# Head 0's queries transposed straight from fp32, and the first mask rows copied in another order

## The chip, the cores and the metric

The kernel runs on one NeuronCore of a Trainium2 chip. Five engines work side by side, each through its own list of instructions in order: TensorE (PE in the profile; its weight loads are PEld), VectorE (DVE), ScalarE (ACT), GpSimd (POOL) and SyncE (SP, which here only issues DMAs). They wait for one another through semaphores. Matrix products go to PSUM, from where VectorE or ScalarE copy them to SBUF. The metric is the device time of one execution in microseconds; three runs of the kernel before gave a median of 210.62 us (210.41 to 210.62).

## What is computed

Block-sparse attention (4 batches, 8 heads, 768 positions, head size 64; blocks of 32 positions) followed by a gated MLP. Cut to what matters:

```python
scores = q @ k.T / sqrt(D)
mask = |blk_i - blk_j| <= 1, or first/last block row or column, or block sampled for that row
attn = softmax(where(mask, scores, -1e9))
x = attn @ v                               # heads side by side: (4, 768, 512)
h = relu(x @ w_in); u, v = halves of h
v_n = (v - mean(v)) / sqrt(var(v) + 1e-6)
v_s = w_spatial @ v_n + b_spatial          # over positions
out = (u * v_s) @ w_out
```

## The kernel before

The 768 positions of a head are held as 6 chunks of 128 (position p*6 + c lies in row p of chunk c). `kq` has one slab for each of 8 heads: in partitions 0 to 63 the transposed keys (columns 0 to 767) and queries (columns 768 on, `Q_`), in partitions 64 and up the mask as extra rows: the keys' side is a one-hot code of the block, the queries' side the row of that block's mask, so that one matrix product gives scores and mask together. `qcols(t)` are the query columns of one third (two chunks, 256 columns).

Heads are taken in pairs. The first batch is worked off in *slots*: slot s makes the transposed scores of a piece (`qk_unit`, L387 to L420), one exponential on ScalarE (L410, L420) turns them into weights, and some slots later `av_unit` multiplies them with v. Score tiles use the PSUM tag `sc` (two buffers of two banks), the first-slot extra `ps_f` and the transposes a pair of banks that `moe_tag()` hands out in turn, `ps_av` and `psq` the tag `av` (two buffers). Slot 0 is head 0 with the first third of queries, made in two halves with an exponential each (L407, L410); slot 1 is head 0 with the second third, slot 2 head 0 with the last two key chunks for both thirds, slots 3 to 5 the same for head 1; from slot 6 on come pairs 1 to 3. The order on each engine is the order in which the program text issues the work: `tc.manual_schedule()`, no planner. `at`, `pre` and `late` hang further work on slots: `second` and `third` (L331, L337) transpose the rest of pair 0, `tr_first(p)` and `tr_rest(p)` pairs 1 to 3.

The start, which the change touches:

- DMAs: ScalarE's queue brings keys (four chunks) and then queries (four chunks) of head 0 as fp32 (L140, L141). SP's queue brings the other two chunks of keys, then head 1's keys and queries (L143 to L145), then pairs 1 to 3 and the first weights in the order of `ORDER`.
- GpSimd makes index patterns (`iota`), the bf16 identity (L169), the ones beside v (L171) and zeros in head 1's first query columns (L173); then it casts to bf16 head 0's queries (L245), the rest of pair 0 (L246 to L248), copies mask rows (L301, L302), and casts what `ORDER` brings (`casts`, L321).
- ScalarE casts head 0's first keys (L243), copies the keys' mask rows from slab 1 to slab 0 (L244), and then the queries' mask rows of the first two thirds from PSUM (`mask_rows`, L268, called at L290 and L298), with a copy of mask rows into head 2 between them (L291).
- VectorE builds the mask, copies transposed keys and queries from PSUM into `kq` (`split0`, L280: one half of a bank's partitions, two chunks at a time) and copies mask rows to other heads (`rows`, L236).
- TensorE runs 26 small products on zeros (`filler`), transposes head 0's first keys (`head`, L274), makes the mask rows, transposes head 0's queries into `psq` (L294), and starts slot 0.

The cast for pair 0 also reorders chunks, so that chunk pairs (0,2) and (1,3) are transposed together and each half of the partitions then holds two neighbouring chunks, one third of the queries.

Of the kernel before, what the change touches and what calls it, by code (L numbers as in the profile page):

```python
# [10 lines left out]
FP32 = mybir.dt.float32  # L11
# [15 lines left out]
def kernel(  # L27
# [16 lines left out]
    nc = tc.nc  # L44

    B, H, S, D = q.shape
# [16 lines left out]
    TC = NCH // NT  # L63
    TW = TC * 128
# [5 lines left out]
    const = ctx.enter_context(tc.tile_pool(name="const", bufs=1))  # L70
    work = ctx.enter_context(tc.tile_pool(name="work", bufs=1))
    psum = ctx.enter_context(tc.tile_pool(name="psum", bufs=1, space=bass.MemoryType.PSUM))
    ctx.enter_context(tc.manual_schedule())

    ident = const.tile([128, 128], BF16)
    warm = const.tile([128, 128], BF16)
    w_in_t = const.tile([128, NDM, DFF], BF16)
    w_out_t = const.tile([128, NDH, DM], BF16)
# [4 lines left out]
    kq = const.tile([128, H, 2 * S], BF16, name="kq")  # L83
    NVV = 6
    vv = [const.tile([128, 2, NCH, VA], BF16, name=f"vv{s}") for s in range(NVV)]
    MR = slice(D, KR)
    MX = slice(D, 128)
    K_, Q_ = slice(0, S), slice(S, 2 * S)

    def qcols(t0, n=1):  # L90
        return slice(S + t0 * TW, S + (t0 + n) * TW)


    st = {}
# [6 lines left out]
    H0, H1, BOTH = slice(0, 1), slice(1, 2), slice(0, 2)  # L101
    ALLC, C01, C03, C45 = slice(0, NCH), slice(0, TC), slice(0, 2 * TC), slice(2 * TC, NCH)
# [12 lines left out]
    def nat0_view():  # L115
        return nat[0].rearrange("p c h d -> p (c h d)").rearrange("p (h x) -> p h x", h=2)

    def cast(p, nm, eng, hs=BOTH, cs=ALLC):
        if nm == "v":
            dst = vv[p % NVV][:, hs, cs, 0:D]  # L120
        else:
            if p not in nat:
                nat[p] = work.tile([128, 2 * NCH, 2, D], BF16, tag="nat", bufs=4, name="nat")
            c0 = 0 if nm == "k" else NCH
            dst = nat[p][:, c0 + cs.start:c0 + cs.stop].rearrange("p c h d -> p h c d")[:, hs]
        src = st[nm, p].rearrange("p h (c d) -> p h c d", d=D)[:, hs, cs]
        if p == 0 and nm != "v":
            dst = nat0_view()[:, hs, (c0 + cs.start) * D:(c0 + cs.stop) * D]
            if cs is not C45:
                dst = dst[:, 0].rearrange("p (i t d) -> p t i d", t=2, d=D)  # L130
                src = src[:, 0].rearrange("p (t i) d -> p t i d", t=2)
            else:
                dst = dst.rearrange("p h (c d) -> p h c d", d=D)
        if eng is nc.scalar:
            nc.scalar.activation(out=dst, in_=src, func=AF.Copy)
        else:
            eng.tensor_copy(out=dst, in_=src)  # L137
# [23 lines left out]
    def iota(out, pattern, base, mult):  # L161
        nc.gpsimd.iota(out, pattern=pattern, base=base, channel_multiplier=mult,
                       allow_small_or_imprecise_dtypes=True)
# [2 lines left out]
    iota(edge[MR], [[0, 1]], 1 - NB, 2)  # L166
    iota(hot[MX], [[2, NCH], [2 * NCH, 128]], 1 - BLK, -2 * BLK)
    iota(col[MR], [[0, NR], [1, NB]], 0, 0)
    make_identity(nc, ident)  # L169
    for s in range(NVV):  # L170
        nc.gpsimd.memset(vv[s][:, :, :, D:VA], 1.0)  # L171
    nc.gpsimd.memset(mhalf, -0.5)
    nc.gpsimd.memset(kq[0:D, 1, 0:TW], 0.0)  # L173

    wps = psum.tile([128, 512], FP32, tag="av", bufs=2)

    def filler(n, to):
        for _ in range(n):
            nc.tensor.matmul(out=to[:, 0:128], lhsT=warm, rhs=warm, start=True, stop=True)
# [28 lines left out]
    PL, DV = nc.gpsimd, nc.vector  # L208
# [4 lines left out]
    def act_copy(o, i):  # L213
        nc.scalar.activation(out=o, in_=i, func=AF.Copy)
# [21 lines left out]
    def rows(hs, cs, eng=nc.vector):  # L236
        src = kq[MX, 0:1, cs].to_broadcast([MX.stop - MX.start, hs.stop - hs.start, cs.stop - cs.start])
        if eng is nc.scalar:
            nc.scalar.activation(out=kq[MX, hs, cs], in_=src, func=AF.Copy)
        else:  # L240
            eng.tensor_copy(out=kq[MX, hs, cs], in_=src)

    cast(0, "k", nc.scalar, H0, C03)  # L243
    act_copy(kq[MX, 0, K_], kq[MX, 1, K_])  # L244
    cast(0, "q", PL, H0, C03)  # L245
    cast(0, "k", PL, H0, C45)  # L246
    cast(0, "k", PL, H1)
    cast(0, "q", PL, H1, C03)  # L248
# [4 lines left out]
    def moe_tag():  # L253
        moe_tags.rotate(1)
        if moe_tags[0] in held:
            moe_tags.rotate(1)
        return moe_tags[0]

    def bank(nm="ps", tag=None):
        return psum.tile([128, 1024], BF16, tag=tag or moe_tag(), bufs=2 if tag else 1, name=nm)  # L260
# [7 lines left out]
    def mask_rows(ps, t, copy, h=0, rs=slice(0, KR)):  # L268
        nc.tensor.matmul(out=ps[:, 0:TW], lhsT=bm[rs], rhs=kq[rs, h, t * TW:(t + 1) * TW],
                         start=True, stop=True)  # L270
        copy(kq[MX, 0, qcols(t)], ps[0:MX.stop - MX.start, 0:TW])


    def head(ps, h, c0, n, at=0):  # L274
        for i in range(0, n, 2):
            nc.tensor.transpose(out=ps[:, at + i * 64:at + (i + 2) * 64],
                                in_=nat0_view()[:, h, (c0 + i) * D:(c0 + i + 2) * D],
                                identity=ident)

    def split0(ps, h, c0, n, t, copy=dve_copy):  # L280
        w = n * 64
        copy(kq[0:D, h, c0 * 128 + t * w:c0 * 128 + (t + 1) * w], ps[t * D:(t + 1) * D, 0:w])

    K4, K2, Q4 = (0, 2 * TC), (2 * TC, NCH - 2 * TC), (NCH, 2 * TC)
# [3 lines left out]
    rows(slice(3, 4), K_)  # L288
    filler(FILL2[0], wps)
    mask_rows(psum.tile([128, 1024], FP32, tag="sc", bufs=2, name="mq"), 0, act_copy, 1)  # L290
    rows(slice(2, 3), slice(0, 512), nc.scalar)  # L291
    filler(FILL2[1], wps)
    psq = bank("psq", "av")
    head(psq, 0, *Q4)  # L294
    split0(psq, 0, *Q4, 0)
    split0(ps0, 0, *K4, 1)
    filler(FILL2[2], wps)
    mask_rows(psum.tile([128, 512], FP32, tag=moe_tag(), bufs=1, name="mq"), 1, act_copy, rs=MR)  # L298
    split0(psq, 0, *Q4, 1)
    rows(slice(4, 6), K_)  # L300
    rows(H1, qcols(0, 2), PL)  # L301
    rows(slice(2, 3), slice(512, S), PL)  # L302

    ORDER = ("k1 q1a v00 v01 k2 q2a v1 k3 q3a v2 q1b q2b r v3 q3b q0c w00 w01 w02 w03 w10 w12 w11 w13").split()
    PIECE = {"k": {}, "v": {}, "q": {}, "a": {"cs": C01}, "b": {"cs": C25}, "c": {"cs": C45},
# [592 lines left out]
```

## Time and profile before

| | |
|---|---|
| median of three runs | 210.62 us (210.41 to 210.62) |
| the profiled execution's own time | 210.04 us |
| its span, first to last instruction | 208.3 us |
| granted TensorE clock, mean | 1.000 |
| chain that ended last, by engine | PE 87%, DVE 4%, ACT 4%, DMA 2% |
| queries of head 0 land | 4.34 us |
| first score product starts | 5.68 us |
| first exponential starts | 6.11 us |

Times inside the execution are microseconds from the start of the span. In lines of the timeline the first two numbers are start and length; `x4` says that four instructions are merged in the line, and the bracket how long the engine was idle before it and what ended that. In the two lines of slices each digit is the busy share of a fortieth of the span in tenths. `nat` is the bf16 copy of keys and queries, `st_q`, `st_k`, `st_v` are the landed fp32 tiles, `ps` and `psq` PSUM tiles, `mq` the product that makes mask rows, `a_all` the exponentials.

### The profile page before, as it was taken

To read this page: it belongs to the slowest core of one execution; us is meant where nothing else is said; L and a number is where in the kernel's file an instruction comes from. 1 tells how busy PE (TensorE), PEld (TensorE's weight loads), DVE (VectorE), ACT (ScalarE), POOL (GpSimd) and SP (SyncE) were. 2 spreads that over 40 slices of the span, in tenths; PEclk is the share of its full clock that TensorE was granted. 3 is DMA by queue.
4 is the path that set the end of the run, shared out by engine and by line. 5 is a ranking of instruction groups with operands and counts; after the bars stand their busy time and mean duration, and the time that the engine had idled before them with its cause. 6 is when DMAs were issued, how large, how long until landed. Compare 5 with 4: busy or idle time off the path is not lost.

```text
span 208.3 us, 5489 instructions
## 1 busy us (share of the span) xinstructions
PE 201.0 (97%) x2203; PEld 138.0 (66%) x2225; DVE 146.8 (70%) x315; ACT 168.4 (81%) x222; POOL 89.4 (43%) x186
## 2 busy tenths in 40 slices
PE   6899999999999999999999999999999999999993
PEld 6599888777766776667556676667665567445551
DVE  6888776989876766575975585456875666576871
ACT  6899999999999999989899878889899884266021
POOL 6888989767927964006757600006210000013000
PEclk9999999999999999999999999999999999999999
DMA  5999899999999999499987920499402010610016
GB/s 143 338 362 357 275 383 270 206 247 389 253 253 308 259 300 208 139 199 386 292 176 206 139 41 0 164 189 335 75 0 41 0 37 4 250 57 0 0 70 232
DMA packets 53053, 39.48 MB, mean 190 GB/s; under 512 B 33956, under 2 KB 47652, under 8 KB 53028
## 3 DMA queue, kind: packets, MB, share of 16 engines
q1 hardware_dynamic: 52596, 38.74, 70.0%
q10 hardware_dynamic: 432, 0.39, 0.6%
q8 instruction: 17, 0.28, 0.5%
q14 instruction: 8, 0.07, 0.1%
HBM read 24.77 MB, written 6.29 MB: 149 GB/s over the span
## 4 chain that ended last, share of the span: by engine, by line
PE 87%; DVE 4%; ACT 4%; DMA 2%; issue 1%; POOL 0%; ACTq 0%
PE ps L428 21%; PE ps_moe L630 17%; PE ps_moe L561 13%; PE ps_av L476 12%; PE ps L415 7%; PE ps_av L458 4%; PE ps_t L561 4%; PE ps_t L630 4%; PE ps_sc L630 2%; ACT a_all L420 2%; DVE stats L594 2%; DVE vn L185 2%; DMA st_q<-in_q_dram 2%; PE ps_sc L561 1%; PE ps L263 1%
## 5 line engine op out<-in xcount | busy, mean ns | idle before, releaser
L431 ACT ACTIVATE a_all<-ps 128x768 bf16<-128x768 f32 x144 | 113.4, 812 | 13.8 <-PE ps L428 6.2
L428 PE MATMUL ps<-kq 128*128 128x512 bf16 (+1 forms) x288 | 70.3, 326 | 0.3
L476 PEld LDWEIGHTS <-a_all 128*128 128x128 bf16 x864 | 46.6, 98 | 19.0
L476 PE MATMUL ps_av<-vv,a_all 128*128 128x65 bf16 x864 | 51.1, 194 | 0.1
L428 PEld LDWEIGHTS <-kq 128*128 128x128 bf16 x288 | 27.9, 97 | 23.6
L137 POOL CAST nat<-st_k 128x256 bf16<-128x256 f32 (+3 forms) x37 | 17.7, 509 | 38.7 <-DMA st_k<-in_k_dram 38.7
L420 ACT ACTIVATE a_all<-ps 128x1024 bf16<-128x1024 f32 x35 | 33.5, 1027 | 0.3
L630 PE MATMUL ps_moe<-w_spt,vn 128*128 128x512 bf16 (+1 forms) x144 | 33.1, 325 | 0.0
L598 POOL TENSOR_SCALAR std<-mv 128x3 f32<-128x3 f32 (+1 forms) x9 | 3.4, 376 | 48.7 <-DVE mv L595 48.5
L661 DVE TENSOR_TENSOR sb<-ps_moe,b_row 128x512 f32<-128x512 f32 x18 | 12.4, 690 | 14.5 <-PE ps_moe L630 14.2
L630 PE MATMUL ps_moe<-xt,w_in_t 128*128 128x256 bf16 (+1 forms) x108 | 21.7, 299 | 0.2
L415 PE MATMUL ps<-kq 128*128 128x256 bf16 x135 | 20.8, 275 | 0.8 <-DVE kq L211 0.6
L561 PE MATMUL ps_moe<-w_in_t,xt 128*128 128x512 bf16 x65 | 20.2, 378 | 0.2
L137 POOL CAST vv<-st_v 128x256 bf16<-128x256 f32 (+2 forms) x37 | 18.5, 533 | 3.9 <-DMA st_v<-in_v_dram 3.8
L137 POOL CAST nat<-st_q 128x256 bf16<-128x256 f32 (+2 forms) x41 | 19.2, 496 | 1.6 <-DMA st_q<-in_q_dram 1.5
L561 PE MATMUL ps_moe<-w_out_t,un 128*128 128x512 bf16 x64 | 19.4, 378 | 0.2
L441 DVE TENSOR_TENSOR xn<-ps_av,rc 128x384 bf16<-128x384 f32 (+1 forms) x36 | 18.5, 513 | 1.4 <-DVE rc L440 0.2
L664 DVE TENSOR_TENSOR un<-sb,un 128x512 bf16<-128x512 f32 x24 | 17.4, 727 | 1.5
L630 PEld LDWEIGHTS <-vn 128*128 128x128 bf16 x192 | 15.5, 97 | 4.4
L594 DVE BATCH_NORM_STATS2 stats<-vn 128x6 f32<-128x512 bf16 x24 | 16.5, 688 | 1.5 <-ACT vn L589 0.9
L211 DVE COPY osb<-ps_moe 128x512 f32<-128x512 f32 x12 | 8.3, 689 | 11.2 <-PE ps_moe L561 9.3
L211 DVE COPY kq<-tt 64x1536 bf16<-64x1536 bf16 x24 | 15.4, 641 | 0.6 <-DMA tt<-nat 0.2
(94 smaller groups left out, 241.6 us busy)
## 6 DMA issues: line engine op xcount, KB each, us to landing
out_dram<-osb SPq DMA_DIRECT2D x23, 256.0 KB, 2.1
st_k<-in_k_dram SPq DMA_DIRECT2D x15, 384.0 KB, 4.6
st_v<-in_v_dram SPq DMA_DIRECT2D x15, 384.0 KB, 6.2
st_q<-in_q_dram SPq DMA_DIRECT2D x12, 384.0 KB, 4.9
ws_f<-in_moe_w_spatial_dram SPq DMA_DIRECT2D x6, 384.0 KB, 5.5
w_f<-in_moe_w_in_dram SPq DMA_DIRECT2D x8, 256.0 KB, 6.3
w_f<-in_moe_w_out_dram SPq DMA_DIRECT2D x4, 256.0 KB, 5.4
st_q<-in_q_dram SPq DMA_DIRECT2D x3, 256.0 KB, 6.9
```

The costliest lines, as they stand in the source:

```text
L137: eng.tensor_copy(out=dst, in_=src)
L211: nc.vector.tensor_copy(out=o, in_=i)
L415: nc.tensor.matmul(out=ps[:, at:at + n * TW], lhsT=kq[:, h, ci * 128:(ci + 1) * 128], rhs=kq[:, h, qcols(t0, n)], start=True, stop=True)
L420: nc.scalar.activation(out=out, in_=ps, func=AF.Exp, scale=0.125)
L428: nc.tensor.matmul(out=ps[:, n0:n1], lhsT=kq[:, j % H, ci * 128:(ci + 1) * 128], rhs=kq[:, j % H, S + n0:S + n1], start=True, stop=True)
L431: nc.scalar.activation(out=a_ref["h", j][:, ci, :], in_=ps[:, 0:S], func=AF.Exp, scale=0.125)
L441: nc.vector.tensor_tensor(out=out, in0=ps[:, :, 0:D], in1=rc[:, 0:n].to_broadcast([128, n, D]), op=ALU.mult)
L476: nc.tensor.matmul(out=av_ref[j][:, qc, :], lhsT=a_ref["h", j][:, ci, qc * 128:(qc + 1) * 128], rhs=vv[p % NVV][:, h, ci, :], start=(ci == ...
L561: nc.tensor.matmul(out=ref["ps"][:, 0:w], lhsT=lhs(i), rhs=rhs(i), start=(i == 0), stop=(i == n - 1))
L594: nc.vector.bn_stats(out=stats, in_=self.vn[:, tcc, :])
L630: nc.tensor.matmul(out=o.rearrange("p (c t) -> p c t", c=n), lhsT=lhs(i)[:, (d0 + x) * 128:(d0 + x + 1) * 128], rhs=rhs(i), start=(i == 0) ...
L664: nc.vector.tensor_tensor(out=self.in_place(*area), in0=sb, in1=self.in_place(*area), op=ALU.mult)
```

## The change

Head 0's first four chunks of queries are no longer cast. TensorE transposes the fp32 tile itself, against an fp32 identity, into an fp32 PSUM tile; chunks lie in their natural order, so that the first transpose holds chunks 0 and 1 (the first third) in the two halves of the partitions, and the second chunks 2 and 3. Four copies of one chunk each take the place of two copies of two chunks: chunk 1 goes by ScalarE, the others by VectorE. The product for the second third's mask rows is issued before the queries' transposes, from slab 1, into the second `sc` buffer, and not into a bank of `moe_tag()`; its copy is kept back and issued on ScalarE right after chunk 1. ScalarE's copy of 512 columns of mask rows into head 2 goes, and GpSimd's copy there grows from 256 to 768 columns. The bf16 identity is now a cast of the fp32 one, and GpSimd writes the zeros ahead of the ones beside v.

```diff
+    ident_f = const.tile([128, 128], FP32)
...
-    make_identity(nc, ident)
+    make_identity(nc, ident_f)
+    nc.gpsimd.tensor_copy(out=ident, in_=ident_f)
+    nc.gpsimd.memset(kq[0:D, 1, 0:TW], 0.0)
     for s in range(NVV):
         nc.gpsimd.memset(vv[s][:, :, :, D:VA], 1.0)
     nc.gpsimd.memset(mhalf, -0.5)
-    nc.gpsimd.memset(kq[0:D, 1, 0:TW], 0.0)
...
-    cast(0, "q", PL, H0, C03)
...
     mask_rows(psum.tile([128, 1024], FP32, tag="sc", bufs=2, name="mq"), 0, act_copy, 1)
-    rows(slice(2, 3), slice(0, 512), nc.scalar)
+    late_copy = []
+    mask_rows(psum.tile([128, 1024], FP32, tag="sc", bufs=2, name="mq"), 1,
+              lambda *oi: late_copy.append(oi), 1, MR)
     filler(FILL2[1], wps)
-    psq = bank("psq", "av")
-    head(psq, 0, *Q4)
-    split0(psq, 0, *Q4, 0)
+    psq = psum.tile([128, 512], FP32, tag="av", bufs=2, name="psq")
+    for i in range(TC):
+        nc.tensor.transpose(out=psq[:, i * 128:(i + 1) * 128],
+                            in_=st["q", 0][:, 0, 2 * i * D:2 * (i + 1) * D], identity=ident_f)
+
+    def q_part(c, copy):
+        r = c % 2 * D
+        copy(kq[0:D, 0, S + c * 128:S + (c + 1) * 128],
+             psq[r:r + D, c // 2 * 128:(c // 2 + 1) * 128])
+
+    q_part(0, dve_copy)
+    q_part(1, act_copy)
+    act_copy(*late_copy.pop())
     split0(ps0, 0, *K4, 1)
     filler(FILL2[2], wps)
-    mask_rows(psum.tile([128, 512], FP32, tag=moe_tag(), bufs=1, name="mq"), 1, act_copy, rs=MR)
-    split0(psq, 0, *Q4, 1)
+    q_part(2, dve_copy)
+    q_part(3, dve_copy)
     rows(slice(4, 6), K_)
     rows(H1, qcols(0, 2), PL)
-    rows(slice(2, 3), slice(512, S), PL)
+    rows(slice(2, 3), K_, PL)
```

## The prediction

> **What bounds the kernel now.** I began with the page: the busy line and the slices say where an engine is full.
>
> ```profile
> PE 201.0 (97%) x2203; PEld 138.0 (66%) x2225; DVE 146.8 (70%) x315; ACT 168.4 (81%) x222; POOL 89.4 (43%) x186
> PE   6899999999999999999999999999999999999993
> ACT  6899999999999999989899878889899884266021
> ```
>
> From the third slice (10 us) on TensorE hardly has a free moment, and its list of waits after 9 us is empty. Whatever moves the start of that stream moves the end by as much, as long as its inputs keep ahead. The change touches only the first 10 us, so I read the chain of waits there (start, length, what):
>
> ```profile
> 1.14 3.19 DMA st_q<-in_q_dram
> 4.34 0.06 issue
> 4.39 0.57 POOL nat L137
> 4.97 0.04 issue
> 5.01 0.30 PE psq L276 x2
> 5.31 0.02 issue
> 5.34 0.30 DVE kq L211
> 5.63 0.04 issue
> 5.68 0.41 PE ps L407 x2
> 6.08 0.02 issue
> 6.11 1.09 ACT a_all L410 x2
> ```
>
> The queries of head 0 land at 4.34, GpSimd casts them, TensorE transposes, VectorE copies, and the first score product starts at 5.68. The change shortens exactly this chain. But does an earlier first exponential carry on? The exponentials of slots 1 to 4 on ScalarE, then TensorE's products of slot 3:
>
> ```profile
> 7.08 1.03 ACT L420 ACTIVATE a_all<-ps 128x1024 bf16<-128x1024 f32 x1
> 7.98 1.04 ACT L420 ACTIVATE a_all<-ps 128x1024 bf16<-128x1024 f32 x1
> 9.02 1.03 ACT L420 ACTIVATE a_all<-ps 128x1024 bf16<-128x1024 f32 x1
> 9.94 1.02 ACT L420 ACTIVATE a_all<-ps 128x1024 bf16<-128x1024 f32 x1
> ```
> ```profile
> 8.37 0.61 PE L415 MATMUL ps<-kq 128*128 128x256 bf16 x4 [0.57 <-DVE kq L211]
> ```
>
> Starts are 0.90 apart (7.08, 7.98) when ScalarE alone sets them, but 1.04 before slot 3: its products waited for VectorE until 8.37 and ended at 8.98, and the exponential followed at 9.02. So slot 3 is set by VectorE's run of copies, and this run decides what the change is worth:
>
> ```profile
> 5.34 0.28 DVE L211 COPY kq<-psq 64x256 bf16<-64x256 bf16 x1 [0.64 <-PE psq L276]
> 5.65 0.29 DVE L211 COPY kq<-ps 64x256 bf16<-64x256 bf16 x1
> 5.87 0.28 DVE L211 COPY kq<-psq 64x256 bf16<-64x256 bf16 x1
> 6.18 0.56 DVE L241 COPY kq<-kq 64x1536 bf16<-64x1536 bf16 x1
> ```
> ```profile
> 8.03 0.61 DVE L211 COPY kq<-ps 64x256 bf16<-64x256 bf16 x2
> 8.67 0.42 DVE L211 CAST kq<-mq 64x256 bf16<-64x256 f32 x1
> 9.01 0.82 DVE L241 COPY kq<-kq 64x1536 bf16<-64x1536 bf16 x1
> ```
>
> From 5.34 to the copy of head 1's queries that ends at 8.31 and frees slot 3 there is no idle time. Slot 3 therefore moves by what the mask-row copy at 6.18 (the first one that the change leaves as it is) moves.
>
> **The change part by part.**
> *Removed: GpSimd's cast of q and its hand-over.* TensorE takes the landed fp32 data itself, at 4.39 where GpSimd now starts (the same 0.06 after the landing). Before, the transposes started at 5.01: 0.62 earlier. TensorE is idle there for 0.65 us, so nothing is pushed.
>
> *Changed: two transposes in fp32.* No fp32 matmul is in the trace. From below: the bf16 pair, 0.29 (5.01 to 5.30). From above: four times that, 1.16, if elements twice as wide are taken in several passes; twice that again would be out of line with any row. I take 0.48: 0.29 plus two weight loads of 0.097 (TensorE's load row), supposing that wide weights cannot be loaded under the matmul before them; it is nearest to the bf16 row, as the shape and the count are the same. I let the copies wait for both transposes, since all is in one PSUM tile. First copy: 4.39 + 0.48 + 0.04 (PE end 5.30 to DVE 5.34) = 4.91. VectorE is free then: its copy at 4.34 takes 0.36.
> [...]
>
> *Changed: VectorE's copies.* Before, three (two of psq, one of ps0), 0.84 from 5.34 to 6.18. Now four: q chunk 0, ps0's second half, q chunks 2 and 3. A q copy is 64x128 from fp32. VectorE's fp32 rows out of PSUM give 0.558 for 384 elements and 0.424 for 256, so 0.134 for 128; the mask cast of 64x256 is 0.42 long, so 64x128 is 0.285. What counts in a run is start to start: after that cast (8.67) the next began at 9.01, 0.34 later, less 0.134 is 0.21 (bounds: 0.21 and, with the 0.03 gap that bf16 copies leave, 0.32). Four: 0.21 + 0.32 (5.34 to 5.65 is one bf16 copy with its gap) + 0.21 + 0.21 = 0.95. The run of mask rows starts at 4.91 + 0.95 = 5.86 instead of 6.18: 0.32 earlier.
>
> *Moved to ScalarE: q chunk 1, then the second mask rows' copy.* ScalarE loses its 0.61 mask-row copy at 4.57, so it is free from 4.66. Chunk 1 (half of the 0.38 row's elements, about 0.28) runs 4.91 to 5.19, beside VectorE's. The mask copy of 0.38 follows, starting about 0.1 before chunk 1 ends as consecutive rows there do, to 5.5. The products need q at 5.2, start at 5.25 and take 0.43 to the exponential: 5.68 instead of 6.11; the mask copy lies under them. The second mask product is issued earlier, on TensorE's idle time. Slot 1's products follow chunk 3: 4.91 + 0.74 + 0.285 + 0.06 = 6.0, exponential 0.64 later at 6.64, where ScalarE's own run (5.68 + 0.97) has it at 6.65. Slots 2 and 3 by ScalarE: 7.55, 8.46; slot 3 by VectorE: 9.02 - 0.32 = 8.70. VectorE still sets it.
>
> *Moved to GpSimd: the rest of mask rows of head 2.* 768 columns, not 256: a copy of 64x768 is 0.83 in the by-shape rows, the present 64x256 is 0.40: 0.43 more, ahead of the cast of pair 1's k. Before, that cast waited 0.23 for its DMA:
>
> ```profile
> 6.35 1.21 POOL L241 COPY kq<-kq 64x512 bf16<-64x512 bf16 x2
> 7.79 0.82 POOL L137 CAST nat<-st_k 128x768 bf16<-128x768 f32 x1 [0.23 <-DMA st_k<-in_k_dram]
> ```
>
> The present 64x512 copy takes 0.86 under VectorE's 6.18 copy, 0.61 elsewhere; VectorE's copy now ends at 6.4, so 0.25 comes back. Net lateness of the casts about 0; at worst 0.43 - 0.23 = 0.2. The transposes that need them start at 9.51, GpSimd is done with q at 8.96: 0.55 of cover, 0.23 with the shift; if gone, up to 0.2 comes back.
>
> *At GpSimd's start:* the identity in fp32 and a cast to bf16 (0.29, the 128x128 row) put it at about 3.2; its first user on TensorE stands at 3.71 behind the fillers. The zeros go ahead of the ones of v, done by 3.6 for the mask product at 3.97. Bounds: nothing, or 0.1 of lateness if the fp32 steps take half as long again. SP's queue gets and loses no issue; its next loads wait on k's casts, not q's.
>
> **Sum.** Slot 3 and all behind it 0.32 earlier. Against the profiled execution: span 208.3 - 0.3 = 208.0, its time 210.04 - 0.32 = 209.72. That execution lies 0.58 under the median of 210.62; on the median's footing: 210.3. Later feeds have room: pair 2's casts end at 11.36 for transposes at 12.39, pair 3's at 13.96 for 14.48, the first weight cast at 19.91 for a product at 21.23.
>
> **Rivals.**
> 1. *The copy starts behind the first transpose alone.* The tile is one, but the columns differ. First transpose 0.23 + 0.097: copy at 4.76, gain 0.32 + 0.15 = 0.47, so 210.15. More than that is barred: with T as bf16 (0.29 for both) and VectorE free at 4.73 the gain is 0.50, and ScalarE's own run ends gains at about 0.7 (209.9).
> 2. *fp32 is taken in four passes, on TensorE at 4.39 (the other side).* With four times 0.48 = 1.92 the first copy is at 6.35, the mask rows at 7.30, 1.12 late: 211.7; at four times the bf16 pair, 0.36 late: 211.0. It decides from T = 0.80, where the gain is gone. For it: no row shows fp32. [...]
> 3. *The gain stops at another feed.* GpSimd's longer copy collides with VectorE as the 0.82 mask-row copy at 9.01 does now (0.56 alone); pair 1's transposes then hold slot 6 where it is: 210.6.
>
> **How the numbers follow.** Forecast (both transposes waited for, T 0.3 to 0.65): 0.57, time 210.3, own range 210.0 to 210.5. Rival 1: 0.13. Rival 2: 0.18. Rival 3: 0.12. The 0.2% bound, about what a measurement of this kernel can tell from no change, is 0.42 us: 210.20 and 211.04. Faster: 0.25 of the forecast's share (the lower T, shorter copies) and 0.11 of rival 1 make 0.36. Slower: 0.16 of rival 2 and 0.07 of rival 3, which may overshoot, make 0.23. The same: 0.41. Range 209.95 (rival 1 with the shortest copies) to 211.1, which leaves out most of rival 2.
>
> **What would show it.** TensorE's fp32 transposes at 4.39 and their length; VectorE's first q copy at 4.91 and its mask rows at 5.86; slot 3's exponential at 8.70; pair 1's k cast still at 7.8. The prediction is wrong if the transposes take over 0.8, or if slot 3 moves and the exponential of slot 8 (13.72 now) does not.

## The result: 0.43% slower

| | before | after |
|---|---|---|
| median, taken together on the same chips | 210.14 us (209.79 to 210.62, 22 runs) | 211.07 us (210.26 to 211.89, 22 runs) |
| ratio of after to before | | 1.0043, 95% interval [1.0033, 1.0053] |
| the profiled execution's own time | 210.04 us | 210.59 us |
| its span | 208.27 us | 208.82 us |
| first VectorE copy of head 0's queries | 5.34 us | 5.13 us |
| VectorE's copy of mask rows into heads 4 and 5 | 6.18 us, 0.56 long | 6.38 us, 0.91 long |
| exponential of slot 3 | 9.02 us | 9.57 us |

The forecast was 210.3 us on the footing of a 210.62 us kernel, that is 0.32 us faster. Measured is 0.93 us slower by the medians, 0.55 us slower between the two profiled executions. The profile of after is read in the same order as that of before. First the page's busy line and TensorE's and ScalarE's slices:

```profile
PE 202.5 (97%) x2225; PEld 138.4 (66%) x2225; DVE 147.5 (71%) x316; ACT 168.3 (81%) x222; POOL 90.2 (43%) x186
PE   8799999999999999999999999999999999999993
ACT  5899999999999999989899878889899884266021
```

From the third slice on nothing has changed. TensorE's first slice went from 6 to 8 and its second (5.2 to 10.4 us) from 8 to 7, ScalarE's first from 6 to 5. So the loss lies in the first 10 us. There the chain of waits (start, length, what) now reads:

```profile
4.33 0.32 PE mq L270 x2
4.64 0.22 PE wps L181 x2
4.86 0.24 PE psq L298 x2
5.10 0.02 issue
5.13 0.29 DVE kq L213
5.42 0.02 issue
5.44 0.28 ACT kq L216
5.72 0.02 issue
5.74 0.39 ACT kq L216
...
6.27 1.72 POOL kq L243 x2
```

DMA and GpSimd's cast no longer head the chain; TensorE's own queue does. The small products stand in front of the transposes and the chain goes through them without a gap. Then come two copies in turn, VectorE's and ScalarE's, where the prediction had them side by side, and ScalarE's second copy releases GpSimd's copies of mask rows. TensorE's timeline (matmuls):

```profile
4.15 0.49 PE L270 MATMUL mq<-kq,bm 88*128 88x256 bf16 x2
4.58 0.29 PE L181 MATMUL wps<-warm 128*128 128x128 bf16 x2
4.70 0.39 PE L298 MATMUL psq<-ident_f,st_q 128*128 128x128 f32 x2
4.92 0.28 PE L181 MATMUL wps<-warm 128*128 128x128 bf16 x2
5.77 0.38 PE L420 MATMUL ps<-kq 128*128 128x256 bf16 x2 [0.57 <-ACT kq L216]
```

The two fp32 transposes are cheap, 0.39. They start at 4.70, though the queries landed at 4.09 here: both mask products and two small products are ahead of them. VectorE's timeline:

```profile
5.13 0.28 DVE L213 CAST kq<-psq 64x128 bf16<-64x128 f32 x1 [0.27 <-PE psq L298]
5.44 0.29 DVE L213 COPY kq<-ps 64x256 bf16<-64x256 bf16 x1
5.76 0.59 DVE L213 CAST kq<-psq 64x128 bf16<-64x128 f32 x2
6.38 0.91 DVE L243 COPY kq<-kq 64x1536 bf16<-64x1536 bf16 x1
```

Four copies start 0.31, 0.32, 0.30 and 0.32 apart (5.126, 5.441, 5.763, 6.060, then 6.383 for the mask rows): 1.26 in all, where three took 0.84 before. The mask-row copy then takes 0.91 instead of 0.56. On GpSimd's timeline the reason stands beside it: its copies of mask rows start at 6.27, 0.11 ahead of VectorE's. In the kernel before, VectorE's started first, at 6.18 against 6.35. Below, "the collision" is this meeting of the two copies with GpSimd's ahead.

```profile
6.27 1.72 POOL L243 COPY kq<-kq 64x512 bf16<-64x512 bf16 x2 [0.22 <-ACT kq L216]
8.04 0.82 POOL L138 CAST nat<-st_k 128x768 bf16<-128x768 f32 x1
```

The end of VectorE's run still sets slot 3, whose exponential is the first of the two in this line of ScalarE's timeline:

```profile
9.57 1.94 ACT L433 ACTIVATE a_all<-ps 128x1024 bf16<-128x1024 f32 x2 [0.27 <-PE ps L428]
```

From the end of the mask-row copy to slot 3's exponential it is 2.28 in both (6.74 to 9.02, 7.29 to 9.57), and from there to the end of the span 199.25 in both. So the 0.55 can be added up on VectorE alone: first copy 0.21 earlier, run 0.41 longer (1.26 less 0.84), mask-row copy 0.35 longer.

### The profile page after: what moved, and what is told of

Same layout as the page of the kernel before. It is cut to its first block, busy times and chain, and to the rows that moved or that the text cites. A ratio compares the mean times of both kernels' runs of the same rounds, so it can differ in the third digit from the quotient of the medians.

```text
span 208.8 us, 5514 instructions
## 1 busy us (share of the span) xinstructions
PE 202.5 (97%) x2225; PEld 138.4 (66%) x2225; DVE 147.5 (71%) x316; ACT 168.3 (81%) x222; POOL 90.2 (43%) x186
## 4 chain that ended last, share of the span: by engine, by line
PE 95%; ACT 1%; POOL 1%; issue 0%; DVE 0%; ACTq 0%; POOLq 0%
PE ps L441 22%; PE ps_moe L643 19%; PE ps_moe L574 15%; PE ps_av L489 13%; PE ps L428 7%; PE ps_av L471 4%; PE ps_t L574 4%; PE ps_t L643 4%; PE ps_sc L643 2%; PE wps L181 2%; PE ps_sc L574 1%; PE ps L264 1%; ACT a_all L433 1%; POOL kq L243 1%; PE ps_av L264 1%; POOL nat L138 0%
## 5 line engine op out<-in xcount | busy, mean ns | idle before, releaser
L611 POOL TENSOR_SCALAR std<-mv 128x3 f32<-128x3 f32 (+1 forms) x9 | 2.9, 318 | 47.7 <-DVE mv L608 47.5
L643 PE MATMUL ps_moe<-xt,w_in_t 128*128 128x256 bf16 (+1 forms) x112 | 22.9, 302 | 0.0
L574 PE MATMUL ps_moe<-w_in_t,xt 128*128 128x512 bf16 x72 | 22.3, 378 | 0.0
L428 PE MATMUL ps<-kq 128*128 128x256 bf16 (+1 forms) x136 | 20.9, 276 | 1.2 <-POOL nat L138 0.6
L574 PE MATMUL ps_moe<-w_out_t,un 128*128 128x512 bf16 x72 | 21.1, 378 | 0.0
L138 POOL CAST vv<-st_v 128x256 bf16<-128x256 f32 (+2 forms) x37 | 19.1, 548 | 3.7 <-DMA st_v<-in_v_dram 3.3
L138 POOL CAST nat<-st_q 128x256 bf16<-128x256 f32 (+2 forms) x40 | 17.7, 470 | 0.6 <-DMA st_q<-in_q_dram 0.4
L677 DVE TENSOR_TENSOR un<-sb,un 128x512 bf16<-128x512 f32 x24 | 16.8, 700 | 1.5
```

The source lines that it names most:

```text
L428: nc.tensor.matmul(out=ps[:, at:at + n * TW], lhsT=kq[:, h, ci * 128:(ci + 1) * 128], rhs=kq[:, h, qcols(t0, n)], start=True, stop=True)
L574: nc.tensor.matmul(out=ref["ps"][:, 0:w], lhsT=lhs(i), rhs=rhs(i), start=(i == 0), stop=(i == n - 1))
L643: nc.tensor.matmul(out=o.rearrange("p (c t) -> p c t", c=n), lhsT=lhs(i)[:, (d0 + x) * 128:(d0 + x + 1) * 128], rhs=rhs(i), start=(i == 0) ...
L677: nc.vector.tensor_tensor(out=self.in_place(*area), in0=sb, in1=self.in_place(*area), op=ALU.mult)
```

## The experiments

All ratios are to the kernel before, run on the same chip in the same batch; "slot 3" is the start of its exponential, "rows" the start and length of VectorE's first copy of mask rows into heads 4 and 5, both in the one profiled execution.

| run | median us | ratio [95%] | profiled span | rows | slot 3 |
|---|---|---|---|---|---|
| g2_changed_again | 211.13 | 1.0041 [1.0023, 1.0059] | 209.35 | 6.94, 0.90 | 10.12 |
| e4_fp32_alone | 210.70 | 1.0024 [1.0012, 1.0036] | 208.84 | 6.77, 0.56 | 9.60 |
| g0_masks_alone | 210.31 | 1.0006 [0.9986, 1.0026] | 209.01 | 6.31, 1.00 | 9.59 |
| e1_scalar_keeps_rows | 211.14 | 1.0042 [1.0015, 1.0069] | 208.55 | 6.48, 0.56 | 9.31 |
| e2_own_bank | 211.36 | 1.0061 [1.0038, 1.0083] | 209.23 | 6.94, 0.76 | 9.97 |
| e3_rows_after | 210.90 | 1.0047 [1.0022, 1.0072] | 210.59 | 10.66, 0.85 | 10.67 |
| f1_more_filler | 211.15 | 1.0042 [1.0029, 1.0055] | 210.12 | 6.94, 0.91 | 10.13 |
| f2_before_less_filler | 210.78 | 1.0022 [1.0005, 1.0038] | 208.42 | 6.00, 0.93 | 9.20 |
| f3_filler_behind | 210.81 | 1.0025 [1.0014, 1.0036] | 208.35 | 6.26, 0.56 | 9.10 |
| f4_all_mended | 211.91 | 1.0069 [1.0051, 1.0086] | 209.78 | 12.13 and 12.82 | 9.71 |
| g1_masks_behind | 210.59 | 1.0016 [0.9997, 1.0035] | 208.88 | 6.17, 0.93 | 9.38 |
| g3_three_copies | 210.38 | 1.0010 [0.9996, 1.0024] | 208.40 | 5.96, 0.82 | 9.05 |
| h1_same_half_together | 211.04 | 1.0042 [1.0021, 1.0063] | 208.84 | 6.53, 0.56 | 9.53 |
| h2_two_tiles | 210.88 | 1.0026 [1.0007, 1.0045] | 209.30 | 6.80, 0.90 | 9.98 |
| h3_all_found | 210.52 | 1.0011 [0.9998, 1.0025] | 208.69 | 6.12, 0.56 | 8.95 |

An execution's time is its span and some 1.8 us, so the table shows which execution of a kernel was profiled. For e1 and f3 it is the fastest of their runs, for f1 the slowest, for e3 one of four over 212 (the other eight took 210.66 to 210.97). What such a profile shows need not be what the median is made of.

### Which part of the change costs: e4, g0, g2

**e4_fp32_alone** puts the fp32 transposes and four copies, all by VectorE, into the kernel before and leaves its mask rows as they were:

```diff
-    cast(0, "q", PL, H0, C03)
-    psq = bank("psq", "av")
-    head(psq, 0, *Q4)
-    split0(psq, 0, *Q4, 0)
+    psq = psum.tile([128, 512], FP32, tag="av", bufs=2, name="psq")
+    for i in range(TC):
+        nc.tensor.transpose(out=psq[:, i * 128:(i + 1) * 128],
+                            in_=st["q", 0][:, 0, 2 * i * D:2 * (i + 1) * D], identity=ident_f)
+    q_part(0, dve_copy)
+    q_part(1, dve_copy)
...
-    split0(psq, 0, *Q4, 1)
+    q_part(2, dve_copy)
+    q_part(3, dve_copy)
```

> The kernel before with the fp32 transposes alone: no cast, four copies of one chunk, all by VectorE; mask rows, ScalarE's and GpSimd's copies as before. Theory of the prediction (earlier queries shorten the chain, VectorE's run pays two more copies): first product 5.4 and not 5.68, VectorE's mask-row copy at 6.1 and not 6.18, ahead of GpSimd's copy, so 0.56 us long; time 0 to 0.15 under the kernel before. Theory P agrees. Theory F (the fp32 path itself costs the 0.9): time about 211. Theory C: about 0.3 above the kernel before in executions whose clock rises late.

**g0_masks_alone** keeps the cast and the bf16 transposes and makes only the other half of the change:

```diff
-    rows(slice(2, 3), slice(0, 512), nc.scalar)
+    mask_rows(psum.tile([128, 1024], FP32, tag="sc", bufs=2, name="mq"), 1, act_copy, 1, MR)
...
-    mask_rows(psum.tile([128, 512], FP32, tag=moe_tag(), bufs=1, name="mq"), 1, act_copy, rs=MR)
...
-    rows(slice(2, 3), slice(512, S), PL)
+    rows(slice(2, 3), K_, PL)
```

> The kernel before with the other half of the change: cast and bf16 transposes stay, but the second mask product goes ahead into the sc buffer, ScalarE's copy into head 2 goes, GpSimd copies 768 columns. Theory Q (the loss comes with the four fp32 copies on VectorE and with TensorE on the queries' path): no loss here, within 0.15 of the kernel before. Theory G (mask rows and GpSimd's longer copy lose it): 0.4 or more over the kernel before.

**g2_changed_again** is the changed kernel once more, in the batch of g0, g1 and g3.

> The changed kernel again, unaltered, for the spread of its runs beside the others and for a second profile. Theory C: the profile's span is its slot 3 exponential + 199.25 (more only by a later wait that the trace shows), and that exponential is set by when the fp32 transposes end, 5.1 to 5.6 by the time of the clock's rise. Median 211.0 to 211.2.

Measured: the fp32 part alone costs 0.24%; the mask part alone can't be told from nothing; the whole again 0.41%. In e4 the run has five copies, lasts 1.45 (5.324 to 6.770) and is the whole of this profile's loss: its first copy and its mask-row copy (0.56) are as before, and slot 3 is 0.59 later. g0's profile shows the collision (1.00) and a late slot 3, yet its median is level: the profiled execution took 210.78, and the median is 210.31.

The profile of g2 is of another kind than that of after, though the kernel is the same. Its TensorE timeline:

```profile
4.15 0.74 PE L270 MATMUL mq<-kq,bm 88*128 88x256 bf16 x2
4.82 0.39 PE L181 MATMUL wps<-warm 128*128 128x128 bf16 x2
5.01 0.63 PE L298 MATMUL psq<-ident_f,st_q 128*128 128x128 f32 x2
```

VectorE's first copy in g2:

```profile
5.68 0.28 DVE L213 CAST kq<-psq 64x128 bf16<-64x128 f32 x1 [0.69 <-PE psq L298]
```

The same two mask products take 0.74 instead of 0.49, the transposes 0.63 instead of 0.39, and they end at 5.64 instead of 5.09. Small products start 0.107 apart until 5.54 here; in after's profile that ended at 4.15, and from 4.64 on they were 0.055 apart. The trace's record of the granted clock steps up at 5.68 here, at 4.16 in after, at 3.69 in before. Below, "half rate" is the time ahead of this step. So some executions work off the whole queue ahead of the transposes at half rate, and not because the queries come late: they landed at 3.69 in g2 and at 4.09 in after. VectorE's first copy starts at 5.68 instead of 5.13, all behind it is 0.55 later, and the time is 211.12 instead of 210.59. Other profiles with the same queue on TensorE bear this out: the first copy starts at 5.07 to 5.22 where the step is at 3.75 to 4.16 (after, e1, h1), and at 5.68 where it is at 5.68 to 9.55 (e3, f1, g2). After's 22 times lie in three groups (ten at 210.3 to 210.8, seven at 211.05 to 211.24, five at 211.7 to 211.9); the profiles of after and of g2 lie in the first and the second, and the median falls in the second. The step moves from profile to profile: it stands at 3.6 to 6.4 us in 16 of the 17, and at 9.55 in e3's. What sets its moment is not shown. The 0.53 between the two executions is a quarter of a percent, and more than the 0.32 that was to be gained.

### What the mask rows cost: e1, e2, e3, f2, f4

**e1_scalar_keeps_rows** gives ScalarE its 512 columns back, GpSimd has 256 again:

```diff
+    rows(slice(2, 3), slice(0, 512), nc.scalar)
     late_copy = []
...
-    rows(slice(2, 3), K_, PL)
+    rows(slice(2, 3), slice(512, S), PL)
```

> The changed kernel with one part undone: ScalarE again copies 512 columns of head 2's mask rows ahead of the queries (it is idle there for 0.6 us), and GpSimd 256 and not 768. Theory G (the loss is GpSimd's longer copy, 1.16 us, which delays pair 1's k cast and what follows): the k cast starts at 7.8 again, and 0.4 to 0.5 us of the loss of 0.9 comes back, time about 210.6. Theory P (the loss is VectorE's mask-row copy at 6.38, 0.91 us and not 0.56, held up by the GpSimd copy that began at 6.27): that collision is still there, slot 3's exponential stays at 9.5, time within 0.2 of the changed kernel, about 211.0. Theory S (ScalarE's copy of chunk 1 waits for VectorE's copy of chunk 0): no change either.

**e2_own_bank** transposes chunks 0 and 1 a second time, into a tile of its own, from which ScalarE takes chunk 1:

```diff
-    for i in range(TC):
-        nc.tensor.transpose(out=psq[:, i * 128:(i + 1) * 128],
+    psq1 = psum.tile([128, 512], FP32, tag=moe_tag(), bufs=1, name="psq1")
+    for ps_, i in ((psq, 0), (psq1, 0), (psq, 1)):
+        nc.tensor.transpose(out=ps_[:, i * 128:(i + 1) * 128],
```

> The changed kernel, but chunk 1 is transposed a second time into a PSUM bank of its own, from which ScalarE copies it. Theory S: ScalarE's copy starts with VectorE's, at 5.15 and not 5.44, the first product at 5.5 and not 5.77, the first exponential at 5.9 and not 6.18; if that were all of the loss, the time would fall by 0.3 or more, to 210.7 or less. Theory P: the second mask-row copy ends earlier too, so that GpSimd's copy starts at 6.1, still ahead of VectorE's mask-row copy at 6.4, which stays at 0.9 us; slot 3's exponential moves by less than 0.1 and the time by less than 0.1.

**e3_rows_after** moves VectorE's copy of mask rows for heads 4 and 5 behind slot 3:

```diff
-    rows(slice(4, 6), K_)
...
-    ROWS = [(3, 2, 8, qcols(0)), (5, 6, 8, K_),
+    ROWS = [(3, 2, 8, qcols(0)), (3, 4, 6, K_), (5, 6, 8, K_),
```

> The changed kernel with VectorE's mask-row copy for heads 4 and 5 (the one at 6.38) moved behind the copies that slots 2 and 3 wait for. Theory P and the VectorE run of the prediction: the run ahead of slot 3 is 0.94 shorter, slot 2 and slot 3 are then set by ScalarE's own spacing (7.16, 8.06, 8.97 against 9.57), time 0.6 lower than the changed kernel, about 210.5 or less, and its spread over runs shrinks. Theory G: pair 1's k cast and transposes still hold the first slots of pair 1, gain under 0.2. Theory C (TensorE was still at half clock until 4.16 and so late with the transposes): gain under 0.2, since nothing ahead of slot 0 is changed.

None of the three is clearly better than the changed kernel, which was not run in their batch. In e1 the collision is gone from the profile (rows 0.56), but that is the fastest of its nine executions (210.35), and the median, 211.14, hasn't moved. In e2 ScalarE's chunk 1 and VectorE's chunk 0 start almost together:

```profile
5.57 0.28 ACT L216 ACTIVATE kq<-psq 64x128 bf16<-64x128 f32 x1 [0.59 <-PE psq L299]
```
```profile
5.68 0.28 DVE L213 CAST kq<-psq 64x128 bf16<-64x128 f32 x1 [0.63 <-PE psq L299]
```

So in after ScalarE waited for VectorE's copy from the same PSUM tile (5.44, VectorE's ended at 5.41). But the third transpose takes time, GpSimd's copy is ahead by more (6.67 against VectorE's 6.94) and the collision stays. In e3 slot 3 no longer hangs on the mask rows (rows at 10.66, slot 3 at 10.67), but its profile had TensorE at half rate up to 9.55, and the moved copy came back as a wait of TensorE for VectorE, 0.37 at 12.96. That execution took 212.37; whether the faster ones have this wait is not shown.

**f2_before_less_filler** takes the small products between the steps (`FILL2`) from the kernel before: (0, 0, 0) for (2, 2, 2).

> The kernel before without the 6 small products behind the first 26. [...] Theory P: within 0.1 of the kernel before, runs over 211 as rare as there (3 of 30).

The kernel before becomes slower too, by 0.22%, though in the profile its transposes and first copy (5.15 for 5.34) come earlier. Four of the 12 runs are over 211; none of the 29 of the kernel before in that batch is. VectorE's timeline in f2, and GpSimd's:

```profile
5.68 0.28 DVE L211 COPY kq<-psq 64x256 bf16<-64x256 bf16 x1
6.00 0.93 DVE L241 COPY kq<-kq 64x1536 bf16<-64x1536 bf16 x1
```
```profile
5.90 1.29 POOL L241 COPY kq<-kq 64x512 bf16<-64x512 bf16 x2
```

GpSimd is first by 0.1, VectorE's copy takes 0.93, and slot 3 is 0.18 late. The profiled execution is one of the faster ones (210.20); what the ones over 211 lose is not shown. The collision is not the change's own: it hit whichever was second (GpSimd's copy took 0.86 in before, where it began 0.17 behind VectorE's, and 0.61 in after). Over the profiles VectorE's copy took 0.56 where it began first (before 6.18 against 6.35, e1 6.48 against 6.53, f3 6.26 against 6.47, h3 6.12 against 6.23) and 0.76 to 1.00 where GpSimd did (after, e2, f1, f2, g0 to g3, h2). It then ended 0.41 behind GpSimd's first copy, which itself took its 0.61: 6.67 + 0.61 + 0.41 = 7.69 in e2 (7.70 measured), 5.75 + 0.61 + 0.41 = 6.77 in g3 (6.78). In e4 GpSimd's copy was ahead too, but it ended 0.13 after VectorE's began (6.90 against 6.77), and VectorE's kept its 0.56. Casts by GpSimd did the same to later mask-row copies: the prediction's row of 0.82 at 9.01 ends 0.41 behind a cast that ends at 9.41.

**f4_all_mended** combines e1, e2, the small products behind (f3) and a later place for the mask rows, slot 5:

```diff
+    ROWS = [(3, 2, 8, qcols(0)), (5, 4, 6, K_), (5, 6, 8, K_),
```

> The changed kernel with everything suspected undone at once: products on zeros behind the queries' transposes (0, 0, 10), chunk 1 in a bank of its own, ScalarE keeps 512 columns of head 2's mask rows, VectorE's mask rows of heads 4 and 5 at slot 5. If the causes named (clock, serial copies, VectorE's run, GpSimd's longer copy) are all there is, the earlier queries show at last: first product 5.3 to 5.5, slot 3's exponential 8.5 to 8.8, time 0.2 to 0.5 under the kernel before, 209.6 to 209.9. If the time is at or over the kernel before, a cause is missing.

The expectation was missed widely. The rate rose at 5.86 in this profile, the three transposes ended at 5.65, the first copy is again at 5.68, and slot 3 comes at 9.71 and not at 8.5 to 8.8. Then more is lost. TensorE's timeline, then VectorE's:

```profile
15.31 0.61 PE L429 MATMUL ps<-kq 128*128 128x256 bf16 x4 [0.68 <-DVE kq L213]
```
```profile
12.12 1.86 DVE L243 COPY kq<-kq 64x1536 bf16<-64x1536 bf16 x2
14.02 0.18 DVE L454 RECIPROCAL rc<-ps_av 128x4 f32<-128x4 f32 x1
14.24 0.42 DVE L455 TENSOR_TENSOR xn<-ps_av,rc 128x256 bf16<-128x256 f32 x1
14.58 1.40 DVE L213 COPY kq<-ps 64x1024 bf16<-64x1024 bf16 x2
```

Two mask-row copies in a row, beside GpSimd's casts, hold VectorE for 1.86, the transposed keys and queries of a pair are copied only at 14.58, and the products that need them stall. VectorE had no more room there than ahead of slot 3.

### What stands ahead of the transposes: f1, f3, g1

**f1_more_filler** and **f3_filler_behind** are the changed kernel with other counts of small products: `FILL2` (2, 2, 10) and (0, 0, 10) for (2, 2, 2). **g1_masks_behind** is f3 with the second mask product issued after the transposes.

> The changed kernel with 10 and not 2 of the small products on zeros behind the queries' transposes (8 more, nothing else). [...] Theory P (the loss is copies that meet on VectorE and GpSimd, whatever the clock): the products only stand in TensorE's way, median 211.1 or more and the same spread up to 211.9.

> The changed kernel with no small products ahead of the queries' transposes and 10 behind them. Theory C (even in the faster runs TensorE, still at half clock, works off masks and small products until 4.6 to 5.0, and not 4.39, before it takes the queries): transposes start 0.2 to 0.4 earlier in executions whose clock rises after 4.4, and the median is 0.1 to 0.3 under that of the same kernel with the products ahead (first run of this set). Theory P or theory S (ScalarE's copy waits for VectorE's): no difference between the two.

> The changed kernel with small products (0, 0, 10) and the second mask product behind the queries' transposes: ahead of them TensorE has only one mask product left. By the sum read from the traces so far (slot 3's exponential = start of VectorE's first query copy + 1.26 + mask-row copy of 0.56, or 0.91 where GpSimd's copy came first, + 2.28; span = that + 199.25): with the transposes at 4.4 to 4.5 the first copy is at 4.85 (clock up) to 5.1 (half clock), slot 3 at 8.95 to 9.2, or 9.3 to 9.55 with the collision; times 210.0 to 210.5, median 210.3, few runs over 210.7. If the half clock is not what spreads the changed kernel's runs, the median stays at 210.8 or more with runs up to 211.8.

More of them behind the transposes does nothing (f1: 211.15, and the spread stays). With none of them in front the median is lower: 210.81 (in f1's batch, though the intervals overlap), and 210.59 with the mask product behind too. The transposes end at 4.96 and 4.87 in these profiles, and TensorE is no longer behind in its queue. So of the 0.9 us some 0.5 was the queue ahead of the transposes, by the medians of one batch (211.13 in g2, 210.59 in g1, whose profile still has the collision). The two intervals overlap a little, so that this is likely and not proven.

### The run of copies: g3, h1, h2, h3

**g3_three_copies** is g1 with chunks 0 and 2 in one copy of 64x256 and chunk 1 in a tile of its own for ScalarE, so that VectorE has three copies again:

```diff
-    q_part(0, dve_copy)
+    dve_copy(kq[0:D, 0, S:S + 512].rearrange("d (c t n) -> d c t n", c=2, t=2)[:, :, 0],
+             psq[0:D, 0:256].rearrange("d (c n) -> d c n", c=2))
...
-    q_part(2, dve_copy)
```

> As the kernel with masks behind, and VectorE makes three copies instead of four (chunks 0 and 2 in one, 64x256), chunk 1 in a bank of its own for ScalarE. By the same sum with 1.09 in place of 1.26: slot 3 at 8.75 to 9.2, time 209.8 to 210.2, that is 0.1 to 0.2 under the kernel with four copies and at or under the kernel before. If VectorE's run did not set slot 3, no difference between the two.

The run is 0.98 long and the kernel is level with the one before (and with g1, of the same batch, by the intervals), though the collision is still in its profile. In its timeline of VectorE a copy starts before the one ahead has ended (5.43 + 0.29 is 5.72):

```profile
4.98 0.42 DVE L213 CAST kq<-psq 64x256 bf16<-64x256 f32 x1
5.43 0.29 DVE L213 COPY kq<-ps 64x256 bf16<-64x256 bf16 x1
5.64 0.29 DVE L213 CAST kq<-psq 64x128 bf16<-64x128 f32 x1
```

So an fp32 copy can follow at 0.21. What decides it? **h1_same_half_together** changes nothing but the order of VectorE's copies in the changed kernel:

```diff
+    q_part(2, dve_copy)
     split0(ps0, 0, *K4, 1)
     filler(FILL2[2], wps)
-    q_part(2, dve_copy)
     q_part(3, dve_copy)
```

> Only the order of VectorE's copies is changed: q chunk 0, q chunk 2, second half of the keys' tile, q chunk 3. The first two read PSUM partitions 0 to 63, the last two 64 to 127; in the changed kernel the halves alternate. Theory S: a copy starts about 0.08 before the one ahead of it ends when both read the same half and write the same half, else 0.01 to 0.03 after it. Then spacing is 0.21, 0.31, 0.21, 0.32 and the run from the first q copy to the mask rows 1.05 rather than 1.26; slot 3's exponential is 0.2 earlier, at first copy + 1.05 + the mask-row copy (0.56 alone, 0.91 behind GpSimd's) + 2.28; median about 210.9 where the changed kernel has 211.1. Theory L: fp32 copies take 0.28 to 0.30 each whatever stands ahead, and only the bf16 copy of keys gives 0.21 to the one behind it: spacing 0.30, 0.31, 0.21, 0.32, run 1.14, median about 211.0. Theory W: the gaps are waits for ScalarE's copy of chunk 1 from the same tile: the second copy then starts no earlier than 0.04 after ScalarE's ends, run 1.3 or more.

VectorE's timeline in h1:

```profile
5.07 0.28 DVE L213 CAST kq<-psq 64x128 bf16<-64x128 f32 x1 [0.30 <-PE psq L298]
5.70 0.28 DVE L213 CAST kq<-psq 64x128 bf16<-64x128 f32 x1 [0.34 <-ACT kq L216]
6.00 0.29 DVE L213 COPY kq<-ps 64x256 bf16<-64x256 bf16 x1
6.21 0.28 DVE L213 CAST kq<-psq 64x128 bf16<-64x128 f32 x1
```

Both theory S and theory W are right in part. Chunk 2 waited for ScalarE's copy of chunk 1 from the same tile (ended 5.66), as W has it: the run is 1.45, and nothing is won. And behind the keys' copy, which reads the upper half, chunk 3, which reads the upper half too, follows at 0.21.

**h2_two_tiles** transposes chunks 2 and 3 into a second PSUM tile (the loop's `out=(psq, psq1)[i][...]`).

> The two fp32 transposes go into two PSUM tiles, so that the copy of chunk 0 need not wait for the second. If the wait for both matters (rival 1's other half): VectorE's first q copy starts 0.04 after the first transpose's modelled end (about 0.28 after its start), 0.1 earlier than in the changed kernel at full clock and 0.2 at half clock, and the median falls by that, to 210.9 to 211.0. If it doesn't: the first copy starts behind both transposes, or the gain goes into the serial copies behind, and the median stays at 211.1. Spacing of VectorE's copies stays 0.31, run 1.26.

The first copy starts at 5.54, when the second transpose hasn't ended: the two run from 5.08 to 5.72, at half rate. It begins 0.46 after the transposes' start, where it was 0.67 in g2 (5.01 to 5.68). So in the changed kernel the first copy did wait for a transpose that it doesn't read, and another tile saves 0.2 at half rate. The median is 0.16 to 0.19 under those of h1 and of after, within what these intervals can't tell apart.

**h3_all_found** is g1 with two tiles and the order of h1.

> The changed kernel with the second mask product and the small products behind the transposes (as in g1_masks_behind, median 210.59), two PSUM tiles, and the copies ordered by half. Theory S: first copy at 4.9 to 5.0 (VectorE's copy ahead of it ends at 4.85), run 1.05, mask rows at 5.95 to 6.05, 0.9 long behind GpSimd's, slot 3's exponential at 9.15 to 9.25 against 9.38 in g1: median about 210.4, level with the kernel before (210.28). Theory L: 0.1 later, 210.5.

VectorE's timeline in h3:

```profile
5.09 0.48 DVE L213 CAST kq<-psq 64x128 bf16<-64x128 f32 x2
5.58 0.29 DVE L213 COPY kq<-ps 64x256 bf16<-64x256 bf16 x1
5.80 0.29 DVE L213 CAST kq<-psq 64x128 bf16<-64x128 f32 x1
6.12 0.56 DVE L243 COPY kq<-kq 64x1536 bf16<-64x1536 bf16 x1
```

The two fp32 copies from the lower half take 0.48 together here (starts 0.21 apart), 0.59 in after's profile, where lower and upper follow each other. The run is 1.03, as theory S has it (1.05). Slot 3's exponential comes at 8.95, earlier than in the kernel before (9.02). Yet the span is 208.69: a wait further on has taken its place. VectorE's and GpSimd's timelines some slots later in h3:

```profile
11.64 1.09 DVE L243 COPY kq<-kq 64x1536 bf16<-64x1536 bf16 x1
12.76 0.18 DVE L454 RECIPROCAL rc<-ps_av 128x4 f32<-128x4 f32 x1
12.97 0.42 DVE L455 TENSOR_TENSOR xn<-ps_av,rc 128x256 bf16<-128x256 f32 x1
13.31 1.40 DVE L213 COPY kq<-ps 64x1024 bf16<-64x1024 bf16 x2
```
```profile
11.48 0.83 POOL L138 CAST vv<-st_v 128x768 bf16<-128x768 f32 x1
```

The next mask-row copy took 0.56 at 11.59 in the kernel before; now GpSimd's cast of v starts 0.15 ahead of it and it takes 1.09. The transposed data of a pair is copied 0.28 later (13.31 for 13.03), and TensorE, which never waited there before, starts the next products at 14.04, where an unbroken queue would have at 13.73 (the eight products ahead take 0.26 from start to start one step earlier). A second loss of 0.18 follows at 24 us (point 1 below). No version beats the kernel before; g3 and h3 are level with it.

## Why the prediction was wrong, step by step

1. **What bounds the kernel: right.** VectorE's run sets slot 3, and slot 3 the end, one to one: 199.22 to 199.26 from slot 3's exponential to the end in before, after, e1, e2, e4, f2, f3 and g2. In f1, f4, e3 and h3 (199.7 to 200.1) a new wait of TensorE some slots later is seen in the trace. In g0, g1 and h1 (199.31 to 199.50) the loss is at 24 us: VectorE's copy of 64x1024 mask rows at 21.3 to 21.5, beside GpSimd's casts of weights, took 0.79, 0.85 and 0.68 where it took 0.61 in before, and the exponential there is 0.18, 0.24 and 0.08 later (h3: 0.78 and 0.18). The 0.09 of g3 and the 0.06 of h2 are not explained. Neither of the two signs of being wrong that the text named came: the transposes stayed under 0.8, and slot 8's exponential moved with slot 3's (13.72 to 14.28).
2. **Two fp32 transposes, 0.48: right in size, not in its reason.** 0.39 in after, 0.63 at half rate. The two loads of 0.097 that the 0.48 holds beside the bf16 pair are shown by no run: in after the loads took 0.14 each, and the second (4.71 to 4.85) lies under the first transpose (4.70 to 4.98). Rival 2 (four passes) falls. Its factor of four and that of the upper bound were the author's supposition; in after the fp32 transposes start 0.116 apart, the small bf16 products 0.055. Rival 1 falls for one tile: the first copy started 0.04 after the second transpose (5.09 to 5.13); h2 shows that it holds with two.
3. **Transposes at 4.39, "TensorE is idle there for 0.65 us, so nothing is pushed": wrong.** They started at 4.70. The idle time before them in the old profile was made by the late cast, and it covered the queue ahead of it. With the cast gone, the second mask product (0.28) and the small products stand in the way, and where the rate rises late it is 5.01. First copy 0.21 earlier, not 0.43.
4. **The four copies, 0.95 from start to start: wrong, and enough by itself to take away the gain.** It measured 1.26, 0.31 more, and the forecast gain was 0.32. The text had both prices for an fp32 copy, 0.21 and 0.32, and took 0.21 from the mask cast at 8.67 and its follower at 9.01. That row was a special case: the cast writes the upper half of `kq`'s partitions, and so does its follower. In the kernel before, 5.65 and 5.87 are 0.22 apart, and both read the upper half; 5.34 and 5.65 are 0.31 apart, lower and upper. The change's order is lower, upper, lower, upper, and then mask rows from SBUF: 0.31 each time. h3, which pairs the halves, measured 1.03. In the traces of before, after, e2, e4, g3, h1 and h3, from the first q copy to the copies of 10.2 us, a copy that reads or writes another half than the one ahead starts 0.013 to 0.033 after that one's end, if no other engine keeps it, and one that reads and writes the same halves 0.08 before it. The mask cast's follower is the exception: it starts 0.08 before too, though the cast reads the lower half, of PSUM, and the follower the upper one, of SBUF. At 0.283 + 0.03 four copies of the first kind make 1.25. In the medians this price is not resolved: g1, g3 and h3 can't be told apart.
5. **ScalarE's chunk 1 beside VectorE's chunk 0: wrong.** It came after it, 5.44 behind 5.41, because both read one PSUM tile; with a tile of its own it ran beside (5.57 and 5.68 in e2, 4.93 and 4.98 in g3). So in after the first exponential was at 6.18 and not 5.68, and ScalarE's mask copy, which releases GpSimd, ended at 6.12 and not 5.5.
6. **The mask-row copy, 0.56, "VectorE's copy now ends at 6.4", before GpSimd's: wrong, and the largest miss.** A later VectorE met GpSimd's copy, which was earlier than in before: 6.38 against 6.27, and 0.91. Rival 3 named the collision of these two engines, but at GpSimd's longer copy, and with no loss.
7. **The sum.** Predicted 0.43 + (0.84 - 0.95) = 0.32 earlier. Measured on the same steps: 0.21 earlier, 0.41 and 0.35 later, 0.55 late in all, which is the difference of the profiled spans. So the steps that failed are 3, 4 and 6: they missed by 0.22, 0.31 and 0.35, 0.87 in all between 0.32 early and 0.55 late. The rest of the 0.93 between the medians is likely executions such as g2's.
8. **What came near by luck.** The range 209.95 to 211.1 holds 211.07, and rival 2's lower time, 211.0, lies beside it. But that end of the range stands for transposes in several passes, 1.16 long, which did not happen. And the kernel before measured 210.14 here and not 210.62: on that footing the forecast is 209.82, 1.25 under the result.

Two things are open: how the 0.9 us of the median splits between the late rise of the rate, the longer run and the collision, since each kernel has one or two profiles; and what after's third group of times (211.7 to 211.9) is. The profile of f1 at 211.92 shows two more waits of TensorE at 40.8 and 42.5 us, and that of e3 at 212.37 a rate that rose only at 9.55, but those are other kernels.

## What to carry to other kernels

When a wait is taken away, look at what it hid: here the products queued ahead of the transposes, and the order in which the mask-row copies of two engines met (GpSimd's 6.35 behind VectorE's 6.18 in before, 6.27 ahead of 6.38 in after). Cost a run of short copies by their starts, and look which half each reads and writes before a spacing is carried from one pair of rows to another; ordering copies of like halves together was worth 0.1 us per pair here (0.21 from start to start in h3, 0.31 in after), but nothing in h1, where another engine copied from the same tile in between. A gain in a start that is tuned to 0.1 us can shift later meetings of two engines: h3 won 0.07 at slot 3, lost 0.3 at the next mask-row copy and 0.18 at one further on.

## What was not expected of the hardware

- Two fp32 transposes of 128x128 started 0.116 apart at full rate (after) and 0.214 at half rate (g2), bf16 products of that shape 0.055 and 0.107: twice as far, not four times. One was 0.28 long in after, the bf16 product 0.22.
- The rate of TensorE rose anywhere from 3.6 to 9.55 us after the start of the span with the same 26 small products ahead, and with it one kernel's time moved by 0.5 us between two executions (210.59 and 211.12).
- VectorE's mask-row copy was not stretched in proportion where GpSimd's had begun first: it ended 0.41 after GpSimd's first copy, whether it began at 5.96 (g3), 6.38 (after) or 6.94 (e2) (0.56 alone, 0.76 to 1.00 behind it), while the GpSimd copy took its 0.61. Where GpSimd's ended only 0.13 after VectorE's start (e4), nothing was lost.
